# Splitting the rows of x and w1 so that heads h and h+4 share a transfer, and merging before turning B and K, in an RWKV-7 recurrence followed by a mixture of experts

## The chip, the cores and the metric

The kernel is one program on one core of a Trainium2 chip. The core has five engines that run their own instruction streams beside each other: TensorE (PE, matrix products; PEld is its weight load), VectorE (DVE), ScalarE (ACT), GpSimd (POOL) and SyncE (SP, which here only issues DMA transfers). The metric is the device time of one execution in microseconds, the median of several runs; lower is better.

## The reference

```python
# attention: B, H, S, D = 4, 8, 768, 40
state = np.zeros((B, H, D, D))
for t in range(S):
    kt, vt, rt = k[:, :, t], v[:, :, t], r[:, :, t]
    wt, at, bt = w[:, :, t], a[:, :, t], b[:, :, t]
    y[:, :, t] = einsum('bhd,bhde->bhe', rt, state)
    Sa = einsum('bhde,bhe->bhd', state, at)
    state = state * wt[:, :, None, :] - einsum('bhd,bhe->bhde', Sa, bt)
    state = state + einsum('bhd,bhe->bhde', vt, kt)

x = y.transpose(0, 2, 1, 3).reshape(B * S, H * D)      # 3072 x 320

# mixture: 4 experts, w1 (4, 320, 1024), w2 (4, 1024, 320)
p = domain_probs / (domain_probs.sum(-1, keepdims=True) + 1e-09)
for e in range(E):
    h = np.maximum(x @ w1[e], 0.0)
    out += p[:, e:e + 1] * (h @ w2[e])
```

The output is 3072 x 320, all in float32.

## The kernel before

**Tiles and units.** The 768 steps are cut into NC = 12 chunks of L = 64 tokens. One *unit* u is one chunk of two of the four batches, so there are NU = 24 units, two to a chunk (`q.c` is the chunk, `q.bp` says which two batches). Within a chunk the recurrence is turned into products of matrices and a triangular system. Two units together make one chunk of the mixture's input, and the mixture of that chunk is computed during the next two units: its products (`ph`, `p`) fill TensorE between the short products of the recurrence. A stretch of the mixture that goes with one unit is called a *window* in what follows; the windows of odd u are those at whose head a fresh piece of w1 is read.

**One unit's chain.** The decays are accumulated (G, a scan, L559) and inverted (gp, L575). Raw A, B and K are turned so that channels lie on partitions. For units from `BY_CHANNEL` = 8 on, B and K are turned on VectorE straight from the raw tiles: two transposes each into NT and KT (L318, called from L627 to L637), and one product each with gp (L633, L637). TensorE forms scores (`pfe`, `pc`), ScalarE copies them (F, L662), `substitute` (L709 to L777) puts F's diagonal blocks in `blocks` (L714), transposes them into M (L726), and solves 32 steps of a triangular system in Z. From unit 2 on these steps run on GpSimd (L756, L773). Then `merge` (L779) transposes Z twice on VectorE: Qc (L784) and QTc (L785); GpSimd copies QTc into QT (L791). `two_heads` multiplies QTc with `below` on TensorE (pY); what follows from it (pQ, psat, pdy) gives the unit's Y and the new state.

**Y and xT.** Y has the shape [128, 4, 2, 64]: head h of the eight lies on partitions 64*(h%2) to 64*(h%2)+39, in pair j = h // 2 of its second axis; the last two axes are batch and token. The mixture wants x the other way: xT is [128, 3, 256], where the 320 features of x lie on partitions in three groups g of 128, 128 and 64, and the third is there twice, on partitions 0 to 63 and 64 to 127. For units 0 to 3 this is done on TensorE by products with a 0/1 matrix `pick` (built by `set_pick` on GpSimd, L164; the pairs of group and Y pair that it covers are `PLACES`, L153). For units 4 to 23 it is done by transfers from SBUF to SBUF on the SP queue (L928 to L939): a head that crosses the border of a group is cut, and what falls in the third group goes twice, which makes 12 transfers for a unit and 240 in all.

**w1 in pieces.** w1 is read in pieces of 640 KB, one expert e and one half x of its 1024 columns each: 37 into the buffer `w1a`, 37 into `w1b`, and 5 early ones into `sums` buffers that later hold sums of w2. `load_piece` (L379) makes three transfers: `main`, rows 0 to 255 as [128, 2, 512], and two `last` transfers of 64 KB each, rows 256 to 319 for one half of the columns each, on partitions 0 to 63 and 64 to 127. The mixture's first product on a piece (`up_last`, L943) multiplies `last` with group 2 of xT, and `up_main` multiplies `main` with groups 0 and 1. All w1 pieces go through SP in program order, between the loads of the raw inputs, the xT transfers and the stores of the output.

**What sets the order.** TensorE's stream is in program order through most of the program, so what a wait holds up holds up all behind it. VectorE's stream is given by a list of names and pairs (L1426 to L1439): each pair says which instruction stands before which. `ahead_of_merge` is one of these lists; before the change it puts the product K of unit u before Qc of unit u-1, and QTc of u-1 before RH of u-1 and VC of u. SP issues strictly in program order. Two pieces of w1 are held back by hand (L1440): one after Y of unit 0, one after SX of unit 5.

Of the kernel before, what the change touches and what calls it, by code (L numbers as in the profile page):

```python
# [33 lines left out]
def kernel(  # L34
# [38 lines left out]
    nc = tc.nc  # L73

    B, H, S, D = r.shape
    E, DM, F = moe_w1.shape
    P = 128
# [3 lines left out]
    NJ = H // 2  # L81
    NF = F // P
    NU = NC * B // 2
    DT = DM - 2 * P
# [5 lines left out]
    def noted(ins, name, n=None, i=None):  # L90
        if n is None:
            n = sum(k.startswith(name) for k in made)
        key = f"{name}{n}" if i is None else f"{name}{n}.{i}"
        made[key] = ins
        if key in names:
            stated_order.append(ins)
        return ins
# [24 lines left out]
    def of_mixture(name):  # L122
# [6 lines left out]
        out=ident[:], in_=ident[:], pattern=[[1, P]], compare_op=ALU.is_equal, fill=0.0,  # L129
        base=0, channel_multiplier=-1,  # L130
# [4 lines left out]
    for t, n, op in ((upf, L, ALU.is_gt), (diagf, Q, ALU.is_equal)):  # L135
        nc.vector.memset(t, 1.0)
        for q in range(P // n):
            o = slice(q * n, (q + 1) * n)
# [11 lines left out]

    PLACES = [(g, j) for g in range(3) for j in range(NJ) if 2 * j * D < (g + 1) * P and 2 * (j + 1) * D > g * P]  # L153

# [7 lines left out]
    def set_pick():  # L164
        nc.gpsimd.memset(pick, 0.0)
        for n, (g, j) in enumerate(PLACES):
            for s in range(2):
                for c in (0, DT) if g == 2 else (0,):
                    w_ = DT if g == 2 else P
                    o = pick[64 * s:64 * s + D, n, c:c + w_]  # L170
                    nc.gpsimd.affine_select(
                        out=o, in_=o, pattern=[[-1, w_]], compare_op=ALU.not_equal, fill=1.0,
                        base=(2 * j + s) * D - g * P, channel_multiplier=1,
                    )

    first = const.tile([P, 2 * NJ, L + 1], FP32, name="first")
# [139 lines left out]
    def turn_raw(out, t):  # L316

        return nc.vector.transpose(  # L318
            out=out.rearrange("p n (x two) -> p n two x", two=2),
            in_=t.rearrange("p n (two e) -> p n two e", two=2)[:, :, :, 0:Q],  # L320
        )
# [57 lines left out]
    def load_piece():  # L379

        (e, x), at, _ = plan[len(pieces)]
        if isinstance(at, int):
            t = sums[at]
        else:
            t = sb.tile([P, PIECE], FP32, name=at, tag=at)
        q = Piece()
        q.main = t[:, 0:2 * HF * P].rearrange("p (g c) -> p g c", g=2)
        q.last = t[:, 2 * HF * P:PIECE].rearrange("p (f c) -> p f c", c=P)
        cols = slice(x * HF * P, (x + 1) * HF * P)
        moves = [(q.main, moe_w1[e, 0:2 * P, cols].rearrange("(g p) c -> p g c", p=P))]  # L390
        for i in range(2):
            half_cols = slice((2 * x + i) * HF // 2 * P, (2 * x + i + 1) * HF // 2 * P)
            moves.append(
                (q.last[i * DT:(i + 1) * DT], moe_w1[e, 2 * P:DM, half_cols].rearrange("d (f c) -> d f c", c=P))
            )
        for n, (to, src) in enumerate(moves):
            ins = nc.sync.dma_start(out=to, in_=src)
            tc.keep_in_program_order(ins)
            if n == 0:
                noted(ins, "piece")  # L400
        pieces.append(q)
# [92 lines left out]
    def within(q):  # L494
# [131 lines left out]
        if by_channel:  # L626
            NT = sb.tile([P, 2 * NJ, L], FP32, name="NT", tag="turned", bufs=3)  # L627
            KT = sb.tile([P, 2 * NJ, L], FP32, name="KT", tag="turned", bufs=3)
            for t, x in ((NT, "B"), (KT, "K")):
                for i in range(2):  # L630
                    turn_raw(t[:, i::2], n["raw" + x][:, NJ * i:NJ * i + NJ])
                if x == "B":
                    nc.vector.scalar_tensor_tensor(  # L633
                        out=t[:], in0=t[:], scalar=-1.0, in1=gp[:], op0=ALU.mult, op1=ALU.mult,
                    )
                else:
                    noted(nc.vector.tensor_tensor(out=t[:], in0=t[:], in1=gp[:], op=ALU.mult), "K", q.u)  # L637
# [179 lines left out]
    def step(q, xT):  # L817
# [102 lines left out]
        if placed:  # L920
# [4 lines left out]
                    start=(n == 0 or PLACES[n - 1][0] != g), stop=(n + 1 == len(PLACES) or PLACES[n + 1][0] != g),  # L925
                )
            nc.scalar.copy(out=xT, in_=px[:, 0:3 * P].rearrange("p (g t) -> p g t", g=3))
        for h in range(0 if placed else H):  # L928
            lo = h * D
            while lo < (h + 1) * D:  # L930
                g, o = divmod(lo, P)
                hi = min((h + 1) * D, (g + 1) * P)
                at = 64 * (h % 2) + lo - h * D
                for to in (o, o + DT) if g == 2 else (o,):
                    nc.sync.dma_start(
                        out=xT[to:to + hi - lo, g, :],
                        in_=Y[at:at + hi - lo, h // 2].rearrange("p i t -> p (i t)"),
                    )
                lo = hi  # L939
        yield  # L940

    def up_last(k, xT, n):
# [484 lines left out]
    turned_ahead = [("Qc6", "RT7"), ("RT7", "QTc6")]  # L1427
    turned_ahead += [("QTc6", x) for x in ("VC7.0", "VC7.1", "sum_w15", "sum_w16")]
    waits_of_scalar = [(f"SXc0.{n}", "RTc1.0") for n in range(4)]
    ahead_of_merge = [(f"K{u}", f"Qc{u - 1}") for u in range(BY_CHANNEL, NU)]  # L1430
    ahead_of_merge += [(f"QTc{u - 1}", f"RH{u - 1}.{r}") for u in range(BY_CHANNEL, NU) for r in range(2)]
    ahead_of_merge += [(f"QTc{u - 1}", f"VC{u}.{r}") for u in range(BY_CHANNEL, NU) for r in range(2)]
    in_second = [("Zr1.14", "out0"), ("out0", "Zm1.16")]
# [32 lines left out]
```

## Time and profile before

| | us |
|---|---|
| runs before (three) | 1094.92, 1092.51, 1092.59 |
| median | 1092.59 |
| the profiled execution | 1093.63 |
| its span, first to last instruction | 1091.9 |
| TensorE's share | 97% |
| VectorE, ScalarE, GpSimd | 73%, 31%, 48% |
| DMA engines, queue 1 (SP) | 41.7% of 16 engines, 107.76 MB |
| one unit in the steady part | 42.9 to 44.5 |

The profile is of one execution. A row of the groups gives line, engine, operation, output <- inputs, shape and count, then the busy time and the mean of one in ns, then the idle time of the engine just before them and what ended it. A row of waits gives engine, line and what was waited for, then the total in us, the number of times and the longest. A row of the time line gives start and length in us, then the instructions, and in brackets an idle time before them with its releaser. The chain of work that ended last is TensorE for 62% of the span:

```profile
PE 62%; DVE 14%; POOL 12%; issue 4%; DMA 3%; SPq 3%; ACT 1%; DVEq 0%; POOLq 0%; ACTq 0%
```

### The profile page before, as it was taken

To read this page: it belongs to the slowest core of one execution; us is meant where nothing else is said; L and a number is where in the kernel's file an instruction comes from. 1 tells how busy PE (TensorE), PEld (TensorE's weight loads), DVE (VectorE), ACT (ScalarE), POOL (GpSimd) and SP (SyncE) were. 2 spreads that over 40 slices of the span, in tenths; PEclk is the share of its full clock that TensorE was granted. 3 is DMA by queue.
4 is the path that set the end of the run, shared out by engine and by line. 5 is a ranking of instruction groups with operands and counts; after the bars stand their busy time and mean duration, and the time that the engine had idled before them with its cause. 6 is when DMAs were issued, how large, how long until landed. Compare 5 with 4: busy or idle time off the path is not lost.

```text
span 1091.9 us, 38473 instructions
## 1 busy us (share of the span) xinstructions
PE 1055.7 (97%) x16012; PEld 946.9 (87%) x16012; DVE 797.3 (73%) x1565; ACT 343.8 (31%) x942; POOL 524.4 (48%) x1312
## 2 busy tenths in 40 slices
PE   8999999999999999999999999999999999999998
PEld 7787878889889889898888898888988989988888
DVE  7886679897878877868868778678687786543343
ACT  3433344422333323323233333232333332321110
POOL 5116777756366364463572653643735537430000
PEclk9999999999999999999999999999999999999999
DMA  6775643435434453452463453443444443121220
GB/s 119 197 212 114 140 108 107 104 76 112 117 85 102 102 115 91 110 120 62 93 147 71 94 148 65 105 113 85 108 95 109 99 99 95 51 71 56 76 82 13
DMA packets 275989, 111.04 MB, mean 102 GB/s; under 512 B 230456, under 2 KB 255592, under 8 KB 275816
## 3 DMA queue, kind: packets, MB, share of 16 engines
q1 hardware_dynamic: 271832, 107.76, 41.7%
q8 instruction: 126, 2.06, 0.8%
q10 hardware_dynamic: 3984, 0.84, 0.4%
q14 instruction: 47, 0.39, 0.1%
HBM read 100.65 MB, written 3.93 MB: 96 GB/s over the span
## 4 chain that ended last, share of the span: by engine, by line
PE 62%; DVE 14%; POOL 12%; issue 4%; DMA 3%; SPq 3%; ACT 1%; DVEq 0%; POOLq 0%; ACTq 0%
PE ph L110 26%; PE p L110 23%; POOL Z L773 8%; POOL Z L756 4%; PE pdy L110 2%; DVE osb L984 2%; DVE M L726 2%; PE po L110 2%; PE prn L110 1%; PE psat L110 1%; PE pxr L110 1%; DVE a L1095 1%; PE pfe L110 1%; PE pY L110 1%; DVE KT L318 1%
## 5 line engine op out<-in xcount | busy, mean ns | idle before, releaser
L773 POOL TENSOR_TENSOR Z<-Z 128x31 f32<-128x31 f32 (+7 forms) x704 | 258.4, 367 | 55.1
L110 PE MATMUL ph<-xT,w1a 128*128 128x256 f32 (+3 forms) x1536 | 222.8, 374 | 2.8 <-DMA w1a<-in_moe_w_dram 2.0
L110 PE MATMUL ph<-xT,w1b 128*128 128x256 f32 (+3 forms) x1536 | 223.7, 374 | 1.5 <-DVE a L1095 0.5
L1095 DVE TENSOR_TENSOR a<-hs 128x512 f32<-128x512 f32 x220 | 152.2, 710 | 91.8 <-ACT hs L969 91.8
L969 ACT ACTIVATE hs<-ph 128x512 f32<-128x512 f32 (+1 forms) x208 | 116.8, 564 | 324.3 <-PE ph L110 323.9
L110 PEld LDWEIGHTS ph<-xT,w1a 128*128 128x128 f32 (+1 forms) x1536 | 169.4, 161 | 31.8 <-issue 9.0
L110 PEld LDWEIGHTS ph<-xT,w1b 128*128 128x128 f32 (+1 forms) x1536 | 169.9, 161 | 29.0 <-issue 6.4
L756 POOL TENSOR_TENSOR Z<-M,Z 128x62 f32<-128x62 f32 (+7 forms) x352 | 148.6, 422 | 79.7 <-DVE M L742 53.9
L984 DVE SCALAR_TENSOR_TENSOR osb<-p,gate,osb 128x320 f32<-128x320 f32 (+1 forms) x243 | 108.2, 483 | 84.0 <-PE p L110 80.0
L110 PE MATMUL p<-sums,a 128*128 128x160 f32 x1056 | 164.9, 299 | 0.0
L110 PEld LDWEIGHTS p<-sums,a 128*128 128x128 f32 x1056 | 152.8, 190 | 2.2
L719 POOL COPY below<-F 32x256 f32<-32x256 f32 x48 | 22.9, 478 | 201.9 <-ACT F L662 189.7
L110 PEld LDWEIGHTS p<-w,hs 128*128 128x128 f32 x704 | 98.6, 190 | 8.7 <-issue 7.5
L110 PE MATMUL p<-w,hs 128*128 128x160 f32 x704 | 104.9, 302 | 0.1
L110 PE MATMUL p<-w,a 128*128 128x160 f32 x704 | 102.8, 299 | 0.0
L110 PEld LDWEIGHTS p<-w,a 128*128 128x128 f32 x704 | 98.0, 190 | 0.0
L791 POOL COPY QT<-QTc 32x256 f32<-32x256 f32 x96 | 40.3, 420 | 99.2 <-DVE QTc L785 94.2
L889 ACT COPY RS<-pxr 64x256 f32<-64x256 f32 x88 | 32.2, 366 | 100.3 <-DVE SX L492 73.6
L575 DVE RECIPROCAL gp<-G 128x512 f32<-128x512 f32 x16 | 53.6, 3352 | 0.5
L700 ACT COPY EV<-pev 64x160 f32<-64x160 f32 x96 | 23.1, 286 | 83.5 <-PE pev L110 83.1
L726 DVE STREAM_TRANSPOSE M<-blocks 128x1024 f32<-128x1024 f32 x24 | 47.7, 1986 | 1.9 <-ACT blocks L714 0.3
L662 ACT COPY F<-pfe 128x256 f32<-128x256 f32 x48 | 15.6, 376 | 79.3 <-PE pfe L110 78.1
(167 smaller groups left out, 1420.6 us busy)
## 6 DMA issues: line engine op xcount, KB each, us to landing
w1a<-in_moe_w_dram SPq DMA_DIRECT2D x37, 512.0 KB
w1b<-in_moe_w_dram SPq DMA_DIRECT2D x37, 512.0 KB
w<-in_moe_w_dram SPq DMA_DIRECT2D x4, 1280.0 KB
w1a<-in_moe_w_dram SPq DMA_DIRECT2D x74, 64.0 KB
w1b<-in_moe_w_dram SPq DMA_DIRECT2D x74, 64.0 KB
out_dram<-osb SPq DMA_DIRECT2D x45, 80.0 KB
rawW<-in_w_dram SPq DMA_DIRECT2D x48, 72.0 KB
natV<-in_v_dram SPq DMA_DIRECT2D x42, 80.0 KB
```

The source lines that it names most:

```text
L110: return stated(nc.tensor.matmul(**k))
L575: pin(noted(nc.vector.reciprocal(out=gp[:], in_=G[:, :, 1:L + 1]), "1/gp", q.u))
L700: nc.scalar.copy(out=of_slot(q.EV[half(p)], i ^ p)[:, :, 0:D], in_=pev[i][half(p)])
L719: tc.keep_in_program_order(nc.gpsimd.tensor_copy(out=q.below[quarter(i)], in_=q.F[quarter(i), :, 0:Q]))
L726: ins = nc.vector.transpose(out=M[:], in_=cols)
L756: ins = eng.tensor_tensor(out=Z[:, 1:3, 0:n, j + 1:Q], in0=M[:, j:j + 2, None, j + 1:Q].to_broadcast([P, 2, n, m]), in1=Z[:, here, 0:n, j: ...
L773: eng.tensor_tensor(out=z[:, 0], in0=z[:, 0], in1=z[:, x], op=ALU.add)
L791: ins = nc.gpsimd.tensor_copy(out=q.QT[quarter(i), :, quarter(i % 2)], in_=QTc[quarter(i)])
L889: nc.scalar.copy(out=RS[half(s), x ^ s::2], in_=prs[x][half(s)].rearrange("p (j i) t -> p j i t", i=2),)
L969: ins = nc.scalar.activation(out=h[:, i * HF // 2:(i + 1) * HF // 2, 0:n], in_=ph[i][:], func=ACTF.Relu,)
L984: ins = nc.vector.scalar_tensor_tensor(out=to, in0=p, scalar=sc, in1=to, op0=ALU.mult, op1=ALU.add)
L1095: ins = nc.vector.tensor_tensor(out=t[:], in0=x, in1=y, op=op)
```

## The change

It has two parts.

*Rows of x and w1.* The 320 features of x are put in another order in xT. Groups 0 and 1 now hold features 0 to 127 and 160 to 287, and group 2 holds 128 to 159 and 288 to 319. Head h + 4 begins 160 features after head h and lies on the same partitions of Y, two pairs on, so that one transfer can carry both: three transfers of 40 partitions, two pairs and 128 elements, one of 8 partitions, and for group 2 four transfers of 32 partitions (two ranges, each stored twice). That makes 8 for a unit and 160 in all. w1's rows are read in the same order: `main` takes rows 0 to 127 and 160 to 287, and each `last` transfer takes rows 128 to 159 and 288 to 319. The source of a `last` transfer has then two blocks of 32 rows, where it had 64 rows in sequence; the shape on the chip, the bytes and the runs are the same. `pick` gets the same order of features: its selects are 24 for 14 (8 of 40x128 and 16 of 40x32, for 10 of 40x128 and 4 of 40x64), and its products stay six.

*VectorE's order.* In `ahead_of_merge`, the two turns each of raw B and K for unit u (now named `Br` and `Kr`) come after QTc of unit u-1, for u from 8 to 23; before, the product K of unit u came before Qc of unit u-1. In VectorE's stream Qc and QTc then follow directly on the additions to the output that stand before them, and the turns and products of B and K are spread behind VC, RH, G and the scan. From unit 11 on, the turn and multiply of AT stand behind M. The number of VectorE's instructions is the same, and so are the order and number of TensorE's and ScalarE's.

```diff
-    PLACES = [(g, j) for g in range(3) for j in range(NJ) if 2 * j * D < (g + 1) * P and 2 * (j + 1) * D > g * P]
+    HALF, EXTRA = DM // 2, DM // 2 - P
+    RANGES = ((0, 0, 0, P), (1, 0, HALF, P), (2, 0, P, EXTRA), (2, EXTRA, HALF + P, EXTRA))
+
+    def covers(lo, w_, j):
+        return 2 * j * D < lo + w_ and 2 * (j + 1) * D > lo
+
+    PLACES = [(g, j) for g in range(3) for j in range(NJ) if any(covers(lo, w_, j) for i, _, lo, w_ in RANGES if i == g)]
...
-                for c in (0, DT) if g == 2 else (0,):
-                    w_ = DT if g == 2 else P
+                for c, lo, w_ in [(x + to, lo, w_) for x in ((0, DT) if g == 2 else (0,)) for i, to, lo, w_ in RANGES if i == g]:
...
-                        base=(2 * j + s) * D - g * P, channel_multiplier=1,
+                        base=(2 * j + s) * D - lo, channel_multiplier=1,
...
-        moves = [(q.main, moe_w1[e, 0:2 * P, cols].rearrange("(g p) c -> p g c", p=P))]
+        rows = moe_w1[e].rearrange("(g d) c -> d g c", g=2)
+        moves = [(q.main, rows[0:P, :, cols])]
         for i in range(2):
             half_cols = slice((2 * x + i) * HF // 2 * P, (2 * x + i + 1) * HF // 2 * P)
-            moves.append(
-                (q.last[i * DT:(i + 1) * DT], moe_w1[e, 2 * P:DM, half_cols].rearrange("d (f c) -> d f c", c=P))
-            )
+            moves.append((
+                q.last[i * DT:(i + 1) * DT].rearrange("d f c -> d (f c)"),
+                rows[P:HALF, :, half_cols].rearrange("d g c -> g d c"),
+            ))
...
-                    turn_raw(t[:, i::2], n["raw" + x][:, NJ * i:NJ * i + NJ])
+                    noted(turn_raw(t[:, i::2], n["raw" + x][:, NJ * i:NJ * i + NJ]), x + "r", q.u, i)
...
-        for h in range(0 if placed else H):
-            lo = h * D
-            while lo < (h + 1) * D:
-                g, o = divmod(lo, P)
-                hi = min((h + 1) * D, (g + 1) * P)
-                at = 64 * (h % 2) + lo - h * D
-                for to in (o, o + DT) if g == 2 else (o,):
-                    nc.sync.dma_start(
-                        out=xT[to:to + hi - lo, g, :],
-                        in_=Y[at:at + hi - lo, h // 2].rearrange("p i t -> p (i t)"),
-                    )
-                lo = hi
+        def send(to, of):
+            nc.sync.dma_start(out=to, in_=of)
+
+        if not placed:
+            rows = Y[:].rearrange("p j i t -> p j (i t)")
+            for h in range(4):
+                n = min(D, P - h * D)
+                o = 64 * (h % 2)
+                send(xT[h * D:h * D + n, 0:2, :], rows[o:o + n, h // 2::2])
+            o = 64 + D - EXTRA
+            for to in range(0, P, EXTRA):
+                send(xT[to:to + EXTRA, 2, :], rows[o:o + EXTRA, 1 + to // EXTRA % 2 * 2])
...
-    ahead_of_merge = [(f"K{u}", f"Qc{u - 1}") for u in range(BY_CHANNEL, NU)]
+    ahead_of_merge = [(f"QTc{u - 1}", f"{x}r{u}.{i}") for u in range(BY_CHANNEL, NU) for x in "BK" for i in range(2)]
```

## The prediction

> **What bounds the kernel now.** I read the page first, then what TensorE waits for, one unit's passage on three engines, the SP queue where a window of the mixture begins, and the DMA share of the first 100 us.
>
> ```profile
> PE 1055.7 (97%) x16012; PEld 946.9 (87%) x16012; DVE 797.3 (73%) x1565; ACT 343.8 (31%) x942; POOL 524.4 (48%) x1312
> ```
>
> TensorE is busy for 97% of the span, at a granted clock of 0.998, and the change leaves its instructions and their order alone. Only its idle time can shrink, and whatever makes it wait more shows in full. Its waits, grouped by what released it:
>
> ```profile
> PE pY L110 <- DVE QTc L785: 16.9, 16, 1.4
> ...
> PE ph L110 <- DMA w1a<-in_moe_w_dram: 2.0, 3, 1.3
> PE ph L110 <- ACT F L662: 1.3, 2, 0.8
> ```
>
> The first row (total us, times, longest) is the largest: pY waits for VectorE's QTc. Its place in unit 16, VectorE and then TensorE:
>
> ```profile
> 662.10 0.76 DVE L318 STREAM_TRANSPOSE NT<-rawB 128x256 f32<-128x256 f32 x2
> 662.89 0.69 DVE L633 SCALAR_TENSOR_TENSOR NT<-NT,gp 128x512 f32<-128x512 f32 x1
> 663.50 0.77 DVE L318 STREAM_TRANSPOSE KT<-rawK 128x256 f32<-128x256 f32 x2
> 664.30 0.69 DVE L637 TENSOR_TENSOR KT<-KT,gp 128x512 f32<-128x512 f32 x1
> 664.91 0.61 DVE L784 STREAM_TRANSPOSE Qc<-Z 128x256 f32<-128x256 f32 x1
> 665.55 0.45 DVE L785 STREAM_TRANSPOSE QTc<-Qc 128x256 f32<-128x256 f32 x1
> ```
>
> ```profile
> 664.37 0.69 PE L110 MATMUL pc<-RT,VT 40*64 40x64 f32 x32
> 666.14 0.59 PE L110 MATMUL pY<-QTc,below 64*64 64x64 f32 x13 [1.08 <-DVE QTc L785]
> ```
>
> POOL's last Z add ended at 661.92, so Qc could have run at 662.10; 2.8 us of turns and products stand before it, and pY sits idle 1.08. At the head of an odd window SP is the late one (u=13):
>
> ```profile
> 535.23 8.46 SPq L935 DMA_DIRECT2D xT<-Y  x11
> 543.80 1.66 SPq L397 DMA_DIRECT2D w1a<-in_moe_w_dram  x3
> ```
>
> The w1 piece that TensorE wants next is issued behind all of xT, and ph, ready at 547.3, starts at 548.62 (1.30 idle, by w1a). Last, the DMA share early on (from, length, and the rest; share and GB/s end each line):
>
> ```profile
> 30.00:40.00 10.00, 8.57 (x210) 7.13 (x208) 8.18 (x14) 4.83 (x17) 4.51 (x6) 1.00 0.87 218
> 40.00:50.00 10.00, 10.00 (x218) 9.03 (x213) 7.26 (x17) 5.50 (x14) 0.84 (x2) 1.00 0.71 176
> 50.00:60.00 10.00, 10.00 (x86) 7.91 (x83) 9.18 (x33) 2.37 (x8) 0.00 (x0) 1.00 0.91 272
> 60.00:70.00 10.00, 10.00 (x108) 7.81 (x107) 9.38 (x20) 2.93 (x11) 2.41 (x4) 1.00 0.86 234
> ```
>
> The 16 engines are nearly full there, while over the whole span they are 42% busy.
>
> **1. Qc and QTc ahead of the turns.** No instruction is added; 2.8 us of NT and KT work goes from before the merge to after it. In unit 16 QTc would end near 662.10 + 0.61 + 0.45 = 663.2, before pc ends at 665.06, so the 1.08 goes. Over u=10 to 21 the pY waits (the group's 16.9 less 0.41 at u=0, 0.79 at u=7, 1.40 at u=8, 1.07 at u=9) are 13.2 us. What is late next: Z, at u=7 and 8. There VectorE already waits 1.03 for Z at Qc *behind* the turns, which stood in Z's shadow; now VectorE idles 3.9 there and does 2.8 us afterwards. Between Qc7 (274.91) and M of unit 8 (291.66) its only idle time is 1.21 (RH on prn), so M, and the Z chain of 22.8 us behind it, come some 1.6 us later, and u=8, where Z is already the late one, loses about 1.4; u=9, with Z 0.11 short, loses about 0.6 more. At u=10 Z has 2.4 to spare and the lag ends. Net −13.2 + 2.0 = **−11.2** (bounds −14.3, all of u=9 to 21 and no lag, and −8, two lags of 2.8). The AT multiply (0.63), now behind M from u=11, helps odd units, where VectorE reaches `blocks` 0.96 after F (u=17).
>
> NT and KT are now ready some 3 to 7 us later than before (they are spread behind VC, RH, G and the scan), near 670 for unit 17; their reader, pfe, comes at 677.7. Cost nothing; gone if that work slips 7 us. The POOL copies of QT behind QTc start about 2.8 earlier, after an idle of 4.21; nobody waits for them.
>
> **2. xT in 8 transfers.** The 12 issues of a unit take 8.9 us of SP (0.55 to 0.82 each by shape; 8.46 for the 11 above). Eight, by the same rows: 4 × 0.75 + 4 × 0.65 = 5.6, bounds 4.4 and 6.6 by the shortest and longest issue; if a two-range transfer costs two issues, 8.9 again. I take 5.8, so the w1 issues behind it come 2.9 earlier.
>
> **3. w1 by other rows.** The main transfers keep 128 rows of 2 KB runs. The 158 "last" transfers of 64 KB (two to a piece) keep 64 runs of 1 KB, but their source is now two blocks of 32 rows: its outermost count is 2 where it was 64. How a transfer is spread shows in this trace: the 4-byte completion packets on queue 1 number 20,328, and that is the sum over SP's 1344 transfers of the largest number up to 16 that divides the outermost count (64, 32 and 128 rows give 16, 40 give 10, 24 give 12, 8 give 8). No transfer here has different outer counts on its two sides, so the new one is bounded: spread as the nearest row, a w1 last transfer over 16 engines, it costs nothing more; spread by the source's 2, each of two engines gets 32 packets for 4. A 1 KB packet took 50 ns in the median, so the two transfers of a piece put 2 × 28 × 50 ns = 2.8 us more on these two engines. I take the second, since the counts went by divisibility without exception.
>
> [...] No run here shows yet which holds.
>
> *Odd windows.* xT's issue starts just before pY (535.23 against 535.75), behind work of TensorE that ends before the pY wait. So taking the 1.08 away brings ph 1.08 closer to SP. The w1 piece lands 2.9 earlier by part 2 and about 2.5 later by part 3 (2.8, less the part that overlaps): 0.4 earlier, against a need 1.08 earlier. The waits at the heads of the seven odd windows from u=9 now sum to 3.8 (0.27, 0.50, 1.30, 0, 0.78, 0.52, 0.43); each grows by about 0.7, less where there was slack: **+4** (bounds −3.8, all gone, and +9.6, if the eight issues take 6.6 and all seven pay the 0.8).
>
> *The first 100 us.* Eight pieces are issued between 23.75 and 79.04. The last (sums, issued 77.47 to 79.04) landed at about 82.2 and is read at 84.23: 2.0 to spare, and SP issued back to back ahead of it from 60 on. Seven pieces before it add 7 × 2.8 = 19.6 us to two engines. Their free time between 24 and 77 us, by the DMA share of each stretch (0.58, then the four above, then 0.53), is 2.5 + 1.3 + 2.9 + 0.9 + 1.4 + 3.3 = 12.3. Left over 7.3, plus the piece's own 2.8, less 2.0: **+8.1**, at the mixture's ph between 54 and 91 us. Bounds: 0, if SP's issues get out of the way, and 20.4, if none of the free time serves. Work behind it (rawR issued by 72.7 is turned at 86) has 12 us to spare and does not add.
>
> From then on the two engines carry 158 × 28 × 50 ns = 221 us more over the span, 62% busy for 42%; pieces of even windows and raw inputs arrive many microseconds ahead, which hides it.
>
> **4. Choice matrix.** set_pick has 8 selects of 40x128 and 16 of 40x32 for 10 and 4 of 40x64. With 359 ns for the wide and at most 236 for the narrow it is 6.6 us for 4.5 on POOL, ahead of ET's select (done at 18.06; its reader pev starts at 19.42, after warm-up). 2.1 less the 1.4 of slack and a bit: **+0.4** (bounds 0 and 2.1). The six pick products before and after are the same in number.
>
> **Sum**: −11.2 + 4 + 8.1 + 0.4 = +1.3 on the profiled execution of 1093.63 (span 1091.9), which is 1.04 above the median of the three runs shown: 1094.9 there, about 1094 against the median 1092.59.
>
> **Rivals.** *The last transfers stay on 16 engines* (two blocks of 32 rows are 64 packets as before). Then part 3 costs nothing, odd windows lose their waits: −11.2 − 3.8 + 0.4 = −14.6, **1078**. For it: the bytes and runs are the same. Against: the completion counts above.
>
> *The early backlog is larger* (the other side): the padded v and r loads at 30.9 and 35.1 already take SP 4.12 and 3.51 us for two issues each, where others take 0.6, so the queue is at its limit and free time goes to waste behind a full engine. Place: ph and po from 54 to 91 us. At 20.4 the sum is +13.6, **1106**. It decides as soon as the early loss passes 10.1 (then the sum passes +3.3). Against: TensorE has no early wait for a w1 piece in before.
>
> *Z takes the place of the merge's turns in odd units.* pfe comes 1.08 earlier, but VectorE's run up to M starts from output adds before pY and is nearly without idle time, so M does not follow but for the 0.63 of AT. Z's margin at pY of 1.17 (u=15, 17, 19, 21) shrinks to 0.7, at u=11 and 13 (0.18) below nothing. If AT's place doesn't help and VectorE is 1 us late, five odd units keep their 1.08: 5.4 less gain, **1099**. Against: even units have 2 to 3.6 to spare.
>
> **How the numbers follow.** About 0.3% (3.3 us) is what a measurement of this kernel can tell from no change. Chances: the sum as it stands 0.47 (its own range 1087 to 1101: faster 0.13, same 0.14, slower 0.20); spread over 16, 0.20 (faster); early backlog 0.17 (slower); Z in odd units 0.16 (faster 0.02, same 0.02, slower 0.12). Together faster 0.35, same 0.16, slower 0.49. The range 1079 to 1107 reaches to both far cases.
>
> **What would show it.** Right: the group pY <- QTc falls from 16.9 to under 5, with VectorE waiting for Z at Qc7 and Qc8 for some 3.9; packets fall from 275,989 by 2,852 (completion packets: 640 by the fewer xT transfers, counted the same way, and 14 for each of 158 last transfers) to about 273,100; xT issues near 5.8 us per unit; ph waits for sums or w1 between 50 and 92 us by some 8, and for w1a at odd windows by about 1. Wrong: packets that fall by 640 only (16 engines kept), early waits far from 8, or a new group of pY behind Z in odd units.

## The result

The changed kernel takes 1107.65 us in the median (1106.14 to 1108.80), the kernel before 1092.55 measured beside it: a ratio of 1.0126, 95% interval 1.0102 to 1.0150. It is slower by 1.3%, 14 to 15 us. The forecast was 1094, with 1106 as the price of the case on the slow side.

The profiled executions are 1093.63 (span 1091.9) and 1106.14 (span 1104.4), 12.5 us apart. TensorE's row and the DMA packets of the changed kernel, from its page:

```profile
PE 1063.9 (96%) x16012; PEld 950.1 (86%) x16012; DVE 808.8 (73%) x1565; ACT 342.4 (31%) x942; POOL 537.5 (49%) x1322
...
DMA packets 273137, 111.03 MB, mean 101 GB/s; under 512 B 227604, under 2 KB 252740, under 8 KB 272964
```

Two readings. TensorE runs the same 16012 instructions, but is busy 8.2 us longer (1063.9 for 1055.7) and idle 4.3 longer (span less busy: 40.5 for 36.2). And the packets fell by 2,852, to the one, and all of these are completion packets of 4 bytes (17,476 for 20,328): by the prediction's count each last transfer of w1 has 2 of them for 16, which it reads as two engines for sixteen. The sections below speak of engines in this sense; no record names the engine of a packet. What the traces show beside the count is the time: the 128 packets of 1 KB of a piece's two last transfers, where they stand apart from those of other pieces (62 of 79 pieces before, 70 after), take 3.51 us in the median from the first start to the last end, for 1.32 before, though a packet takes 46 ns in the median in both. Of the time in which packets of 1 KB move at all, no more than two move at once in 89%, for 33% before. TensorE's waits in the changed kernel (total us, times, longest):

```profile
PE ph L110 <- DMA sums<-in_moe_w_dram: 8.1, 2, 6.8
PE ph L110 <- DMA w1a<-in_moe_w_dram: 5.1, 6, 1.3
PE ph L110 <- DMA w1b<-in_moe_w_dram: 4.8, 6, 1.4
PE pY L110 <- DVE QTc L792: 3.6, 6, 1.5
...
PE ph L110 <- ACT F L669: 2.0, 3, 0.8
```

The wait that the order was to remove did go: pY fell from 16.9 to 3.6 us, 13.3 less. Waits that the view puts down to w1, in its three buffers, rose from 2.0 to 18.0. (At the odd heads it puts some short waits of ph down to ScalarE's F instead. They stand at the same place and go too once w1 is on time, so they are counted with w1 below.) Here are the two waits at the head of the window of u = 15, from TensorE's time line:

```profile
644.06 0.61 PE L110 MATMUL ph<-xT,w1b 64*64 64x256 f32 x2 [0.44 <-ACT F L669]
646.13 1.27 PE L110 MATMUL ph<-xT,w1b 64*64 64x256 f32 x11 [1.45 <-DMA w1b<-in_moe_w_dram]
```

Where the longer busy time is shows in stretches of the same kernel (from:to, length, TensorE busy and its instructions, granted clock, DMA share, GB/s). These are the same head and what follows:

```profile
645.00:647.00 2.00, 0.87 (x13) 0.87 0.86 244
647.00:649.00 2.00, 2.00 (x64) 0.50 0.46 99
649.00:651.00 2.00, 2.00 (x24) 0.78 0.32 81
651.00:653.00 2.00, 2.00 (x11) 1.00 0.20 41
```

After TensorE has waited 0.44 and 1.45 us within 2.5 us, its clock is granted at one half for 3.41 us. The clock records of the changed kernel show this at 472, 646 and 735 us (3.41 each) and at 90 us (6.83, within the wait of 6.8 that ends at 91.84), besides the one near 25 us and the end, which the kernel before has too. Together that is 17.1 us at half speed. TensorE stands idle for 3.3 of them, so some 6.9 us are lost by them (an estimate, half of the rest), of the 8.2 of longer busy time.

By place, from pY of one unit to pY of another: from the start to unit 2, 113.28 for 104.52 (+8.8); units 2 to 9, 258.62 for 257.77 (+0.9); 9 to 21, 522.87 for 520.84 (+2.0: the six even windows gain 4.5 in all, the six odd ones lose 6.5); 21 to 23, +0.9.

### The profile page after: what moved, and what is told of

It reads as the page before. It is cut to its first block, busy times and chain, and to the rows that moved or that the text cites. A ratio compares the mean times of both kernels' runs of the same rounds, so it can differ in the third digit from the quotient of the medians.

```text
span 1104.4 us, 38446 instructions
## 1 busy us (share of the span) xinstructions
PE 1063.9 (96%) x16012; PEld 950.1 (86%) x16012; DVE 808.8 (73%) x1565; ACT 342.4 (31%) x942; POOL 537.5 (49%) x1322
## 2 busy tenths in 40 slices
DMA packets 273137, 111.03 MB, mean 101 GB/s; under 512 B 227604, under 2 KB 252740, under 8 KB 272964
## 3 DMA queue, kind: packets, MB, share of 16 engines
q8 instruction: 126, 2.06, 0.8%
## 4 chain that ended last, share of the span: by engine, by line
PE 61%; DVE 10%; POOL 10%; DMA 9%; SPq 4%; issue 3%; ACT 1%; ACTq 0%; DVEq 0%; POOLq 0%
PE ph L110 28%; PE p L110 20%; POOL Z L780 6%; POOL Z L763 4%; DMA w1a<-in_moe_w_dram 3%; PE pdy L110 2%; DMA w1b<-in_moe_w_dram 2%; PE po L110 2%; PE psat L110 2%; SPq L936 2%; SPq L301 1%; DVE M L733 1%; SPq L404 1%; DMA sums<-in_moe_w_dram 1%; DVE a L1102 1%
## 5 line engine op out<-in xcount | busy, mean ns | idle before, releaser
L780 POOL TENSOR_TENSOR Z<-Z 128x31 f32<-128x31 f32 (+7 forms) x704 | 255.2, 363 | 55.1
L110 PE MATMUL ph<-xT,w1b 128*128 128x256 f32 (+3 forms) x1536 | 228.0, 378 | 6.5 <-DMA w1b<-in_moe_w_dram 4.8
L1102 DVE TENSOR_TENSOR a<-hs 128x512 f32<-128x512 f32 x220 | 155.4, 725 | 87.4 <-ACT hs L976 87.4
L726 POOL COPY below<-F 32x256 f32<-32x256 f32 x48 | 29.1, 606 | 210.4 <-ACT F L669 164.0
L798 POOL COPY QT<-QTc 32x256 f32<-32x256 f32 x96 | 43.3, 451 | 73.3 <-DVE QTc L792 64.4
```

The costliest lines, as they stand in the source:

```text
L110: return stated(nc.tensor.matmul(**k))
L726: tc.keep_in_program_order(nc.gpsimd.tensor_copy(out=q.below[quarter(i)], in_=q.F[quarter(i), :, 0:Q]))
L780: eng.tensor_tensor(out=z[:, 0], in0=z[:, 0], in1=z[:, x], op=ALU.add)
L798: ins = nc.gpsimd.tensor_copy(out=q.QT[quarter(i), :, quarter(i % 2)], in_=QTc[quarter(i)])
L1102: ins = nc.vector.tensor_tensor(out=t[:], in0=x, in1=y, op=op)
```

## The experiments

The theory after the result: all of the loss, and more, comes from the two engines under the last transfers of w1, through waits early and at the odd heads, and through the clock that falls behind them; the order on VectorE by itself gains. The rivals: the order does not pay, because the odd heads take what pY gives; or the new rows cost in some other way, by SP's queue or the shapes of xT.

### The order alone

```diff
 # the kernel before
-                    turn_raw(t[:, i::2], n["raw" + x][:, NJ * i:NJ * i + NJ])
+                    noted(turn_raw(t[:, i::2], n["raw" + x][:, NJ * i:NJ * i + NJ]), x + "r", q.u, i)
...
-    ahead_of_merge = [(f"K{u}", f"Qc{u - 1}") for u in range(BY_CHANNEL, NU)]
+    ahead_of_merge = [(f"QTc{u - 1}", f"{x}r{u}.{i}") for u in range(BY_CHANNEL, NU) for x in "BK" for i in range(2)]
```

> The kernel before with the new order on VectorE alone (Qc and QTc ahead of the turns of B and K); xT in 12 transfers and w1's rows as before. Theory: the loss of the whole change comes from the w1 last transfers on two DMA engines, so this part alone gains. pY's waits fall from 16.9 to about 3.6 us, as in the changed kernel (-13); at the seven odd windows TensorE comes 1.08 earlier to a piece of w1 that lands no earlier, which gives back about 7 x 0.8 = 5.6. Sum -7.5: about 1085 us. No wait for sums near 84 us. Rival (the order does not pay: what pY gives, the odd windows take): 1090 to 1096.

Measured: 1084.43 us, ratio 0.9933 (0.9910 to 0.9956) against 1092.66: 8.2 less. TensorE's waits:

```profile
PE ph L110 <- DMA w1a<-in_moe_w_dram: 5.3, 3, 3.4
PE ph L110 <- ACT blocks L714: 3.2, 2, 1.7
PE ph L110 <- DMA w1b<-in_moe_w_dram: 2.1, 1, 2.1
...
PE pY L110 <- DVE QTc L785: 1.1, 2, 0.7
```

pY's waits are all but gone (16.9 to 1.1). The waits at the seven odd heads sum to 11.0 (0.86, 0.45, 3.42, 1.55, 1.67, 2.10, 0.98) for 3.8: TensorE comes earlier and w1 does not. At the 3.42 the clock falls for 6.83 us. Nearly half of the gain is given back at the heads; the rest stays. The rival that the order does not pay falls. The run is not quite the changed kernel's half, though: 28 of VectorE's 1565 instructions stand more than two places from where they stand there, turns of raw A and V above all.

### The rows alone

```diff
 # the changed kernel
-    ahead_of_merge = [(f"QTc{u - 1}", f"{x}r{u}.{i}") for u in range(BY_CHANNEL, NU) for x in "BK" for i in range(2)]
+    ahead_of_merge = [(f"K{u}", f"Qc{u - 1}") for u in range(BY_CHANNEL, NU)]
```

> The changed kernel with the old order on VectorE (the product K of a unit ahead of Qc of the unit before): 8 transfers of xT, w1 by the new rows, last transfers from two blocks. Theory: early loss as in the changed kernel (+8.8 from the start to pY of unit 2); pY's waits stay near 16.9, so TensorE comes no earlier to the odd windows and its waits there stay near 4 in sum, with no fall of the granted clock in them. About +9: 1101 to 1102 us. Rival (the order is what costs): 1093 or less. Rival (the two parts do not touch each other, and the order gains 11 in either): 1117 or more.

Measured: 1113.52 us (1106.89 to 1115.47), ratio 1.0184 (1.0145 to 1.0223). The profiled execution is the fastest of the four. Its waits have the early ones as expected and pY's untouched:

```profile
PE pY L110 <- DVE QTc L792: 16.9, 14, 1.7
PE ph L110 <- DMA sums<-in_moe_w_dram: 8.3, 2, 6.8
PE ph L110 <- DMA w1a<-in_moe_w_dram: 2.1, 3, 1.1
```

So the rows cost by themselves, and the waits are where the theory put them. The time is 12 above what was expected, and nearer to the rival at 1117: with the last transfers on two engines the order is worth 5.9 us (1113.5 to 1107.7), for 8.2 in the run before this one. Part of the excess is the clock, which falls for 10.2 us at the early wait here and for 6.8 rather than 3.4 near 23 us; from pY of unit 9 to that of unit 21 the profiled execution is 3.6 longer than before. The other three executions are 5 to 9 us longer than the profiled one; their granted clock, 0.988 to 0.991 for 0.992, accounts for some 1 to 5 of these (an estimate, span times the share not granted), and the rest stays open. Against the kernel before, 10 of VectorE's instructions stand more than two places off, which was not tried alone.

### Sixteen engines by two short transfers each

The last transfers are cut in two of 32 rows.

```diff
 # the changed kernel, load_piece
-            moves.append((
-                q.last[i * DT:(i + 1) * DT].rearrange("d f c -> d (f c)"),
-                rows[P:HALF, :, half_cols].rearrange("d g c -> g d c"),
-            ))
+            for g in range(2):
+                at_g = i * DT + g * EXTRA
+                moves.append((
+                    q.last[at_g:at_g + EXTRA].rearrange("d f c -> d (f c)"), rows[P:HALF, g, half_cols],
+                ))
```

> The changed kernel, but each last transfer of w1 cut in two of 32 rows, so that its outermost count is 32 on both sides: four last transfers to a piece, two more issues (about 1.0 us of SP). Theory: completion packets show 16 engines for each; no wait for sums near 84 to 92 us beyond 3 (SP's extra issues); w1 at odd windows lands 2.9 - 1.0 = 1.9 us earlier than in the kernel before, against a need 1.08 earlier, so its waits fall from 3.8 to about 1; pY -13. Sum about -15 + 0.4, with up to 4 back in the first 100 us: 1077 to 1083 us. Rival (the other rows or xT's shapes cost by themselves): above 1092.

Measured: 1112.69 us, ratio 1.0191 (1.0153 to 1.0229). This missed by 30 us. The early waits are as expected (one of 1.61 for sums at 88 us) and only one head waits for w1 (0.64), but:

```profile
PE pY L110 <- DVE QTc L799: 30.8, 15, 3.2
```

Fifteen pY wait, in VectorE's rows because of this (unit 13):

```profile
508.82 1.42 DVE L728 COPY blocks<-F 32x256 f32<-32x256 f32 x2
510.27 3.35 DVE L589 RECIPROCAL gp<-G 128x512 f32<-128x512 f32 x1
513.54 1.88 DVE L740 STREAM_TRANSPOSE M<-blocks 128x1024 f32<-128x1024 f32 x1
```

With 158 more transfers VectorE's instructions come out in another order; a reciprocal of 3.35 us stands between `blocks` and M, and M, Z and pY are late in turn; at the six longest of these waits the clock falls as well. The packets, 277,879, are within two of what 16 engines for each transfer give (273,137 + 158 × 30). The run says nothing against the theory on engines, and shows that a comparison is clean only if the other engines' orders are the same. The runs below say where that is so.

### Sixteen engines, and nothing else

The third group is dealt out: partition 2d holds feature 128+d and partition 2d+1 holds 288+d. The source of a last transfer is then 32 rows of two each, and its outermost count is 32. The number of transfers and the order of each engine are the changed kernel's.

```diff
 # the changed kernel; pick's selects for the third group take every other column in the same way
-                rows[P:HALF, :, half_cols].rearrange("d g c -> g d c"),
+                rows[P:HALF, :, half_cols],
...
-                send(xT[to:to + EXTRA, 2, :], rows[o:o + EXTRA, 1 + to // EXTRA % 2 * 2])
+                send(xT[to // DT * DT + to // EXTRA % 2:to // DT * DT + DT - 1 + to // EXTRA % 2:2, 2, :], rows[o:o + EXTRA, 1 + to // EXTRA % 2 * 2])
```

> The changed kernel with the third group of features dealt out in turn, but still 8 transfers of xT to a unit; the order of every engine's instructions is the changed kernel's, so the number of engines under the last transfers is the only thing that differs. Theory: completion packets rise by 158 x 14 = 2212 to 275,349; no wait of over 1 us near 90 us; waits for w1 at the odd heads under 2 us in sum (11.1 with xT's and ScalarE's in the changed kernel); the clock stays at 1.00 from 30 us on; pY's waits about as in the changed kernel. 1077 to 1081 us. Rival (the last transfers are not the cause): 1100 or more.

Measured: 1083.27 us, ratio 0.9914 (0.9883 to 0.9946), 24 us below the changed kernel. From its page, and from TensorE's waits:

```profile
DMA packets 275349, 111.04 MB, mean 103 GB/s; under 512 B 229816, under 2 KB 254952, under 8 KB 275176
```

```profile
PE pY L110 <- DVE QTc L792: 8.6, 8, 2.0
...
PE ph L110 <- issue: 1.0, 2, 0.5
```

The packets are those expected, 14 more for each last transfer than in the changed kernel, and no wait is put down to w1 any more, early or at the heads. This settles the main point: how these transfers are spread, with 16 completion packets for 2, is the difference between a loss of 1.3% and a gain of 0.9%. The time is some 2 above the expected range. The first row shows where: with w1 on time, pY waits again, and behind one of these waits (1.95) the clock falls once, which was not expected. What is late is Z, by VectorE's waits:

```profile
DVE Qc L791 <- POOL Z L780: 38.5, 22, 3.6
```

### The same with six transfers of xT

The third group's two ranges can now go in one transfer of 64 partitions each.

```diff
 # the kernel of the run above
-            for to in range(0, P, EXTRA):
-                send(xT[to // DT * DT + to // EXTRA % 2:to // DT * DT + DT - 1 + to // EXTRA % 2:2, 2, :], rows[o:o + EXTRA, 1 + to // EXTRA % 2 * 2])
+            for to in range(0, P, DT):
+                send(xT[to:to + DT, 2, :], rows[o:o + EXTRA, 1::2])
```

> The changed kernel, with the third group of features dealt out in turn: partition 2d holds feature 128+d and 2d+1 holds 288+d. The source of a last transfer is then 32 rows of two each (outermost count 32, with 64 on the chip's side), still one transfer, and xT's third group goes in two transfers of 64 partitions instead of four of 32 (6 for a unit). Theory: 16 engines, no more issues than before, 1.3 us less of SP per unit than in the changed kernel; early waits as before, odd windows nearly without waits, pY -13: -13 - 3.5 + 0.4 = about -16: 1075 to 1079 us. Rival (something else in the rows costs): above 1090. If the count of 32 against 64 does not give 16 engines, it is as the changed kernel, 1100 or more.

> The changed kernel with the third group dealt out in turn and 6 transfers of xT to a unit, once more, for a narrower interval: 1077 to 1081 us, faster than the kernel before and than the changed one. If 1078.7 was a lucky placing of the clock: 1083 or more, as with 8 transfers.

Measured: 1078.74 us, ratio 0.9880 (0.9855 to 0.9905), and again 1079.04, ratio 0.9862 (0.9839 to 0.9885). It beats the kernel before by 1.2 to 1.4% and the changed one by 2.5%. In the first profile pY waits 6.6 us and ph for no transfer; the clock does not fall between 30 us and the end. VectorE's order differs from that of the eight-transfer kernel too, so how much of the 4.5 us between the two is SP's and how much the order's isn't known.

### The rows on sixteen engines, with the old order

> The rows alone, dealt out in turn (8 transfers of xT, last transfers on 16 engines), with VectorE's old order; all orders are those of the run with the rows alone and two blocks (1113.5 us), which differs in the number of engines only. Theory: nothing is lost early, and the waits at the odd heads go (w1 2.9 us earlier, need unchanged): -3.5, +0.4 for the choice matrix. pY's waits stay near 17. About 1089: 1087 to 1091 us. Rival (the other rows cost something apart from the engines): 1095 or more.

The edit is that of the rows alone, on the dealt kernel with eight transfers; all orders are those of the rows alone. Measured: 1084.79 us against 1094.58, ratio 0.9920 (0.9897 to 0.9943), and 29 below the rows alone on two engines. It gained 9.8, more than the 3.5 expected, though the profiled execution is the slowest of the five (1088.62). The stretches from pY to pY show why. Before, two odd windows and the even ones after them:

```profile
535.75:580.29 44.54, 42.16 (x660) 1.00 0.47 113
580.29:623.15 42.86, 41.77 (x661) 1.00 0.41 89
...
796.30:840.28 43.98, 42.39 (x660) 1.00 0.48 114
840.28:883.13 42.85, 41.77 (x660) 1.00 0.40 89
```

With the rows dealt out:

```profile
707.67:750.51 42.84, 41.76 (x661) 1.00 0.52 121
750.51:793.42 42.91, 41.83 (x661) 1.00 0.40 85
```

From unit 9 to 21 the six odd windows of before are 6.0 us longer than the six even ones (263.4 for 257.4), with part of it counted as busy (41.9 to 42.5 for 41.8); with w1 on time the two kinds are equal, but for one pair (44.04 and 44.25) with a pY wait of 2.2 and a fall of the clock. By this the idle time listed at the six heads, 3.4 us, is little over half of what late w1 costs there.

### Two engines, and nothing else

```diff
 # the kernel before, load_piece
-                (q.last[i * DT:(i + 1) * DT], moe_w1[e, 2 * P:DM, half_cols].rearrange("d (f c) -> d f c", c=P))
+                (q.last[i * DT:(i + 1) * DT].rearrange("d f c -> d (f c)"), moe_w1[e].rearrange("(g d) c -> g d c", g=2)[:, P:DM // 2, half_cols])
```

> The kernel before, in all its orders, with one edit: the last transfers read rows 128 to 159 and 288 to 319 of w1, two blocks of 32, as in the changed kernel, while x's third group stays as it was. What is left out: the product of x's third group is taken with other rows of w1, so the output is not the reference's; amounts and shapes are the same. Theory: two engines alone cost. Early +8.8 as in the changed kernel; at the seven odd heads w1 lands 2.5 us later without the 2.9 that eight xT transfers save, so 7 x 2.5 = 17.5 on top of 3.8; waits that long make the granted clock fall at most of them, 7 x 1.7 or more. Sum about +38: 1120 to 1140 us. Rival (two engines cost little, the loss is in the other rows of x or in the order): 1095 or less.

Measured: 1144.34 us, ratio 1.0495 (1.0457 to 1.0533), 53 above. The order of all engines is that of before. Its waits:

```profile
PE pY L110 <- DVE QTc L785: 18.9, 15, 2.7
PE ph L110 <- DMA w1a<-in_moe_w_dram: 14.3, 8, 2.9
PE ph L110 <- DMA w1b<-in_moe_w_dram: 11.2, 7, 3.1
PE ph L110 <- DVE RT L318: 4.9, 1, 4.9
```

Each of the seven odd heads waits 3.2 to 3.9 us (24.5 in sum for 3.8), and the clock falls at every one, and at four other places after 60 us. The place is right; the size was underestimated. The profiled execution (1150.27, one of the two longest of five) is longer than before by 12.1 us up to pY of unit 2, where 8.8 was expected, by 6.5 from unit 2 to 9, where nothing was, and by 38.1 from unit 9 to 23. The rows alone, with the same order of the merge, two engines and eight transfers of xT, take 1113.5: the eight transfers, then, hide a good part of what two engines cost.

### The early pieces alone

The first nine pieces get the two short transfers of 32 rows, the others stay. VectorE's and TensorE's orders are the changed kernel's.

```diff
 # the changed kernel, load_piece
+            if len(pieces) < 9:
+                for g in range(2):
+                    at_g = i * DT + g * EXTRA
+                    moves.append((
+                        q.last[at_g:at_g + EXTRA].rearrange("d f c -> d (f c)"), rows[P:HALF, g, half_cols],
+                    ))
+                continue
             moves.append((
```

> The changed kernel, but each last transfer of the first nine pieces of w1 cut in two of 32 rows; the other pieces as in the changed kernel. VectorE's and TensorE's order stay the changed kernel's. Theory: the early loss comes from the first pieces on two engines. The waits for sums near 92 us (8.1 in the changed kernel) fall to about 1.6, the granted clock does not fall behind them (1.8 us), and all else stays: 8 us below the changed kernel, about 1099 to 1101. Rival (the early loss is SP's, or comes from the new order): within 2 us of the changed kernel, 1106 or more.

Measured: 1095.04 us, ratio 1.0028 (1.0011 to 1.0045) for the changed kernel's 1.0126. The waits for sums fall from 8.1 to 1.0, and the clock stays up where it fell in the changed kernel. That kernel first, then this one:

```profile
84.00:88.00 4.00, 1.05 (x10) 0.85 (x8) 1.80 (x5) 0.84 (x3) 3.30 (x10) 1.00 0.50 88
88.00:92.00 4.00, 0.16 (x1) 0.19 (x2) 3.93 (x8) 0.00 (x0) 3.45 (x8) 0.76 0.78 224
92.00:96.00 4.00, 2.65 (x21) 1.95 (x21) 0.00 (x0) 0.00 (x0) 3.29 (x10) 0.50 1.11 294
```

```profile
84.00:88.00 4.00, 3.02 (x34) 2.48 (x34) 3.86 (x10) 1.45 (x6) 3.44 (x8) 1.00 0.81 240
88.00:92.00 4.00, 4.00 (x85) 3.75 (x84) 2.10 (x4) 0.77 (x2) 3.37 (x9) 1.00 1.20 321
92.00:96.00 4.00, 4.00 (x17) 2.81 (x16) 3.97 (x7) 0.00 (x0) 3.29 (x10) 1.00 0.57 83
```

(After the length: busy time of PE, PEld, DVE, ACT, POOL, then the clock.) The early loss is the pieces' and no one else's: pY of unit 2 comes at 105.06 us for 113.28, which is 8.2 less, as expected. By ratios the whole run gains 10.7 us. The profiled execution, the fastest of eleven, shows where more came from: 4.4 less from unit 9 to 21, with one fall of the clock at an odd head for three. At which heads it falls differs from one kernel to the next with nearly equal waits; the last section sets the falls beside TensorE's idle time.

### Keeping TensorE busy at the odd heads

```diff
 # the changed kernel, up_last
+        for _ in range(4 if k >= 36 and k % 8 == 4 else 0): matmul(out=ph[0][:, 0, :], lhsT=ident[:], rhs=unit_cols[:].rearrange("p a b -> p (a b)"), start=True, stop=True)
         for f in range(HF // 2):
```

> The changed kernel with four idle products of 128x128 by 256 columns (some 0.38 us each, 1.5 together, overwritten by the product behind them) put ahead of ph at the seven odd heads, where TensorE waits 1.5 to 2.1 us for w1. Theory: the three falls of the granted clock between 470 and 740 us come from TensorE's idle time there, so they do not come when it is kept busy: 3 x 1.7 = 5.1 less, while the filler takes the place of most of the wait (11.1 of waits fall to about 2, 10.5 of filler come). About 4 us below the changed kernel: 1101 to 1105. Rival (the clock falls for another reason, or the filler delays ph by its own length): 1108 to 1118.

Measured: 1103.59 us (1102.66 to 1106.07), ratio 1.0106 (1.0077 to 1.0134); the orders are the changed kernel's but for the filler. In the trace each of the four is two products, so that eight stand at a head, some 1.8 us, and they come at nine heads: the last two, at 983 and 1055 us, had no wait to fill. The head whose stretches are shown in the first section, with the filler in it:

```profile
642.00:644.00 2.00, 2.00 (x19) 1.00 0.95 253
644.00:646.00 2.00, 2.00 (x78) 1.00 0.62 143
646.00:648.00 2.00, 2.00 (x11) 1.00 0.23 59
```

The filler adds useless work in place of idle time, and the clock does not fall once between 100 us and the end. From pY of unit 9 to that of unit 21 the profiled execution is 6.4 us shorter than the changed kernel's (516.5 for 522.9); behind unit 23, where filler stands without a wait, it is 3.4 longer. The granted clock over a whole execution is 0.992 to 0.995 in the five of this kernel and 0.987 to 0.990 in the four of the changed one, so the trace shown is no exception: the falls at these heads come from idle time. The intervals of the two ratios overlap; the 4 us between the medians are as expected, but not secured by them.

## Why the prediction was right or wrong

*How the transfers are spread: right, to the packet.* The choice of 2 over 16, from the completion packets of before, gave 273,137, and the dealt kernel's 275,349 fits the same reading with outermost counts of 32 and 64. The nearest row, 64 rows on 16 engines, would have led astray. That all last transfers share the same two engines, on which the sums of 2.8 us for a piece and +8.1 early rest, was the author's estimate and no run shows it; the runs showed 3.51 us for 1.32 for the packets of a piece, and the early waits below.

*The first 100 us: right, +8.1 for waits of 6.79 + 1.35 at the place named and +8.8 in all up to unit 2.* That it came so close is partly luck. The 1 KB packets, read as 50 ns in the median, took 46 in the kernel before, and 55 in the mean; the same sum gives 6.3 with the one and 10.2 with the other. And the clock, half for 6.8 us at that wait, was not in the sum, while a wait of 2.05 at 89 us went away.

*The order, −11.2: about right, by other parts.* pY fell by 13.3 in the changed kernel, and the order alone gained 8.2 net of what the heads took back. In units 10 to 21 pY fell by 10.9 and not by all of its 13.2, for Z is late at some of them (1.46 at u = 21). The lag at units 7 to 9 (2.0) did not come: the waits there fell from 0.79, 1.40 and 1.07 to 0.23, 0.16 and 0.28, and VectorE waited for Z at Qc7 for 1.86, not 3.9:

```profile
284.58 0.62 DVE L791 STREAM_TRANSPOSE Qc<-Z 128x256 f32<-128x256 f32 x1 [1.86 <-POOL Z L780]
```

*xT in 8 transfers: right.* 5.98 us of SP for a unit (5.8 forecast) where nothing stands between them.

*The odd heads, +4: this is the step that failed.* From unit 9 to 21 the prediction's terms come to some −9.8 (pY −13.2, and six sevenths of the +4); measured was +2.0. The waits at the heads rose from 3.8 to 11.1 (1.65, 1.80, 1.72, 1.89, 2.13, 1.49, 0.42), which is +7.3; and at three of the seven the clock fell, 1.7 each, +5.1. The term was mis-sized three times over: the wait's growth by 3 us, the fall of the clock put at nothing without a reason, and the base of 3.8 itself little over half of what late w1 costs, as the run with the old order shows.

The wait's growth was mis-sized where the prediction lets ph come 1.08 closer to SP. In the mean of the seven heads xT's first issue came 2.06 us before pY in the kernel before (at u = 13 at 534.37; the row in the prediction shows the other eleven) and 0.10 before it in the changed one. That is 1.95 closer. So w1's first issue, 7.24 us behind pY before and 6.26 now, came 1.0 earlier against TensorE, where the sum had 2.9 − 1.08 = 1.8. Why it was 1.95 was not tried.

The prediction gives the granted clock as 0.998 and nowhere asks what would lower it. The run with the filler ties the falls to TensorE's idle time (none between 100 us and the end, for three in the changed kernel). In the kernel before, cut as in the last section, no 3.41 us window after 50 us has more than 1.40 of TensorE idle, and the clock stays up.

*The choice matrix, +0.4:* pev waits 0.72 where it had not. The dealt kernel with as many selects has such a wait too (0.75) and still reaches pY of unit 2 at 103.70 (104.52 before), so what it costs in the end can't be told apart.

*The rivals.* Sixteen engines was priced 1078; the kernel that differs in nothing else takes 1083.3. The larger early backlog was priced 1106, near the time that came, but for a cause that was not there, so that agreement is luck: the early waits were as forecast, and the rest came from the clock and the heads. Z as the bound, priced as a small correction, is what VectorE waits for in the better kernels: 38.5 us at Qc with eight transfers, 39.9 with six, for 11.0 before.

## What to carry to other kernels

When a transfer's pattern is changed at equal bytes and runs, count the outermost dimension on both sides and predict the completion packets; here a source of 64 KB written as two blocks, against 64 rows on the chip, had 2 of them, the same data dealt out in turn (32 against 64) had 16, and the two kernels were 24 us apart. A wait of TensorE was dearer here than its idle time: ahead of each of the 32 falls of the clock that the twelve traces have after 50 us it had been idle for 1.62 us or more of 3.41, and behind the two waits at u = 15, 1.89 in sum, it ran at half speed for 3.41 us. Ask of every new wait what stands next to it. Before two kernels are compared for one cause, see that the other engines' instructions stand in the same order in both.

## What the runs showed that was not expected

- The granted clock of TensorE has two values in these traces, 1 and 0.5, and falls last 3.41 us or a multiple (6.83, 10.24), but for the last one, at the end of the trace (1.65 us before, 2.60 in the changed kernel). Within each trace all falls begin whole multiples of 3.413 us apart: in the changed kernel those at 90.09, 472.38, 646.46 and 735.21 come 19, 131, 182 and 208 such windows after the one at 25.24.
- Which waits stand ahead of a fall is not plain from their length, but it is plainer once the twelve traces are cut into these windows and TensorE's idle time in each is added up (by the trace's modelled ends of the products). After 50 us there are 32 falls from full clock; the window ahead of each had 1.62 us or more of idle time (in the changed kernel 3.41, 1.62, 1.89 and 1.73). Of some 3,600 windows without a fall behind them none had more than 1.81 (in the kernel before none more than 1.40), and six had between 1.62 and 1.81. Waits of nearly the same length, cut by these windows or not:

| kernel | waits, us | idle time by window, us | clock |
|---|---|---|---|
| changed, u = 15 | 0.44 and 1.45 | both in 643.05 to 646.46: 1.89 | falls |
| changed, u = 19 | 0.60 and 0.89 | cut at 820.54: 0.68, 0.81 | stays |
| early pieces alone, u = 15 | 0.45 and 1.54 | cut at 633.20: 0.45, 1.54 | stays |
| before, 87 to 89 us | 2.05 | cut at 88.78: 1.36, 0.69 | stays |

- The Z chain on GpSimd, from M's end to Z's end, was 22.08 and 22.80 us in units 7 and 8 before, and 21.49 and 21.53 in the changed kernel, where VectorE idles beside its end. That this is the reason is not shown: in units 21 and 22, where VectorE waits 3.10 and 2.29 for Z in the changed kernel, the chain takes 21.91 and 22.13, for 21.77 and 22.03 before.
- The parts don't add up. On sixteen engines the order alone gives 8.2, the rows alone 9.8 and both together, with eight transfers, 8.2 again (against the medians of before of their own sessions; by their intervals, some 3 us to each side, the three are equal). VectorE's waits for Z at Qc are 28.5 us with the order alone, 6.5 with the rows alone and 38.5 with both. That each part removes another wait, and that Z then holds both together, is read from these waits and was not tested.
